# Hashed attention and two feed-forward blocks on one core: products of weights and VectorE rows change places within a step

## The chip, the core and the metric

The kernel runs on one core of a Trainium2 chip. The metric is the device time in microseconds of one execution. Four compute engines matter here: TensorE (PE, with its weight loads PEld), VectorE (DVE), ScalarE (ACT) and GpSimd (POOL, which here issues DMAs); SyncE (SP) issues the other DMAs. In the trace each engine takes its instructions in the order in which the program lists them, and waits where an operand or a buffer is not ready.

## The reference

Sixteen attention heads (2 batches of 8) over 768 positions with 64 features come first. Queries and keys are hashed to six bits by the signs of a projection; a score counts only where both hashes agree. Then two feed-forward blocks follow on the 1536 tokens with 512 features.

```python
q_bucket, k_bucket = hash(q @ proj), hash(k @ proj)      # 6 sign bits each
scores = where(q_bucket[:, None] == k_bucket[None, :], scale * q @ k.T, -1e9)
attn = exp(scores - scores.max(-1)); attn = attn / (attn.sum(-1) + 1e-9)
x = (attn @ v)                                           # to 1536 x 512
h = x @ w_in; x = (h * tanh(softplus(h))) @ w_out        # 512 -> 2048 -> 512
out = ((x @ w1) * (x @ w2)) @ w3 @ w_out2                # 512 -> 1024 -> 512
```

The large weights arrive as 64-bit floats and are decoded on the chip by one ScalarE and three VectorE operations. Products are made from high and low halves, three matmuls for each.

## The kernel before

The attention part is a hand-written pipeline of steps numbered n = 0, 1, 2, ...; six steps make a group j, and 96 steps (`NS`) hold all scores. A step makes the scores of 128 queries of one head against all 768 keys. What a step issues is fixed by a table `slots`, which `at(n, where, fn)` fills and `run(n, where)` empties, in the order in which the loop (L865 on) names the places. `pin` then ties each engine's instructions to this order, so within the attention part the order on an engine is that of the loop, nearly word for word.

The places and what stands in them:

- `scores` (L533): four matmuls into `ts`, one of two PSUM slots with the tag `s`. `tqk`, `tb` and `w3p` take slots of the same two. `maxima` (L549): VectorE's row maximum of `ts` and a small operation on it. `expo` (L559): ScalarE's exp of `ts` into `E`, with the row sums; it frees the slot.
- `un`: two units a step. A `unit` (L602) is three transposes of `E` into one of two PSUM buffers `et` and a copy to SBUF (`etf`), the first of a step on ScalarE, the second on VectorE (in steps with n mod 6 = 5 both are ScalarE's). `av` (L615): the product with v, into `pv`, in steps with n mod 6 = 2, 3, 4.
- `lv`: VectorE's work that others wait for: `bits_dve` (L506, the mask rows `qa` and `ka` out of `tb`), `norm` (L572, two small operations on the row sums, in steps with n mod 6 = 0), `w3_lo` (L688), `x_out` (L628).
- `pe`: other work of TensorE: `qk_transpose` (`tqk`), `bits_mm` (`tb`; that of q in steps 4, that of k in steps 5 of six), `rb_mm` (L582, `rb`, which spreads the reciprocals that `norm` left, in steps 0 of six), `w3_trans` (`w3p`, steps 24, 30, ..., 66), and two fillers that wait for none of these: `wp_mm` (L697, `wacc`: the product of w3 and w_out2, 24 matmuls a group, spread over steps 26 to 73 by `MM`, six of them in each step 5 of six and four in each step 0 of six) and `h_early` (L352, `hps`: the first matmuls of the feed-forward part, from step 83).
- `la`, `ea`, `ev`, `dm`: ScalarE's and VectorE's other work (splits, decoding, the copies `rb_act`, `w3_hi`, `h_keep`) and DMA issues.

After the last step the feed-forward part runs under a list `prog`; there the framework's scheduler chooses the order on each engine.

Of the kernel before, what the change touches and what calls it, by code (L numbers as in the profile page):

```python
# [34 lines left out]
def kernel(  # L35
# [292 lines left out]
    def h_half(n, j, f, o, m0=0, m1=None):  # L328
        w, xh = weight(n, "wi", j), xhl[n]
        m1 = 3 * KD if m1 is None else m1  # L330
        for m in range(m0, m1):
            kk, i = divmod(m, 3)
            ws, xs = PASS[i]
            nc.tensor.matmul(  # L334
                o, lhsT=w[:, ws, kk, f * 128:(f + 1) * 128], rhs=xh[xs][:, kk, :],
                start=(m == 0), stop=(m == 3 * KD - 1),
            )
# [14 lines left out]
    def h_early(n, j, f, m0, m1):  # L352
        if m0 == 0:
            wh[0] = ps.tile([128, 512], F32, tag="w", name="hps1")
        h_half(n, j, f, wh[0], m0, m1)
# [193 lines left out]
    def maxima(j, i):  # L549
        s = stats[j % 3]  # L550
        nc.vector.tensor_reduce(  # L551
            out=s[:, i, 1:2], in_=sc[j, i][:, :, 0:HS], axis=AX.XY, op=ALU.max, negate=True
        )
        nc.vector.scalar_tensor_tensor(  # L554
            out=s[:, i, 2:4], in0=s[:, i, 1:2].to_broadcast([128, 2]), scalar=THR,
            in1=s[:, i, 0:2], op0=ALU.is_le, op1=ALU.mult,
        )
# [14 lines left out]
    def norm(j):  # L572
        s = stats[j % 3]
        nc.vector.tensor_scalar(
            out=s[:, :, 4], in0=s[:, :, 4], scalar1=1e-9, scalar2=None, op0=ALU.add
        )
        nc.vector.reciprocal(out=s[:, :, 5], in_=s[:, :, 4])
# [74 lines left out]
    def pre_a(nm, i):  # L652
        pre[nm, i] = decode_a(pre[nm, i])
# [43 lines left out]
    def wp_mm(f, n0, n1):  # L697
        if n0 == 0:
            wacc[f] = ps.tile([128, 512], F32, tag="w", name="wacc")
        for n in range(n0, n1):  # L700
            g, s = divmod(n, 3)
            ws, rs = PASS[s]
            nc.tensor.matmul(  # L703
                wacc[f], lhsT=w3t[f][:, ws, g, :], rhs=wo2[rs][:, g, :],
                start=(n == 0), stop=(n == 3 * GT - 1),
            )
# [6 lines left out]

    slots = {}

    def at(n, where, fn):
        slots.setdefault((n, where), []).append(fn)

    def run(n, where):
        for fn in slots.pop((n, where), []):
            fn()
# [28 lines left out]
    for j in range(NJ):  # L752
        s = 6 * j
        for m in range(3):
            for kt in (2 * m, 2 * m + 1):
                at(s + 4 + m, "un", lambda j=j, kt=kt: unit(j, 0, kt))
                at(s + 7 + m, "un", lambda j=j, kt=kt: unit(j, 1, kt))
                at(s + 8 + m, "av", lambda j=j, kt=kt: av(j, kt))
        at(s + 6, "lv", lambda j=j: norm(j))
        at(s + 6, "pe", lambda j=j: rb_mm(j))  # L760
        at(s + 7, "la", lambda j=j: rb_act(j))
        at(s + 11, "lv", lambda j=j: x_out(j))
# [7 lines left out]
    for f in range(GT):  # L770
        n = 24 + 6 * f
        na, nb, nc_ = (n - 6, n - 4, n - 3) if f else (17, 20, 21)
        at(na, "ea", lambda f=f: pre_a(3, f))
        at(nb, "ev", lambda f=f: pre_b(3, f))
        at(nc_, "ev", lambda f=f: pre_c(3, f))
        at(n, "pe", lambda f=f: w3_trans(f))
        at(n + 1, "la", lambda f=f: w3_hi(f))
        at(n + 1, "lv", lambda f=f: w3_lo(f))
        m = 0
        for k_ in range(n + 2, n + 8):  # L780
            m1 = m + MM[k_ % 6]
            at(k_, "pe", lambda f=f, m=m, m1=m1: wp_mm(f, m, m1))
            m = m1
        assert m == 3 * GT
        at(n + 8, "la", lambda f=f: wp_out(f))
# [20 lines left out]
    n = 83  # L806
    for jj in range(3):
        for f in range(2):
            m = 0
            while m < 12:  # L810
                m1 = min(12, m + (4 if n % 6 in (2, 3, 4) or n == 83 else 8))
                at(n, "pe", lambda jj=jj, f=f, m=m, m1=m1: h_early(0, jj, f, m, m1))
                m = m1
                n += 1
            at(n, "la", lambda jj=jj, f=f: h_keep(0, jj, f))
# [49 lines left out]
    for n in range(max(NS + 6, HEND + 2)):  # L865
        j, i = divmod(n, 6)
        mark = len(nc.cur_bb.bb.instructions)
        run(n, "pr")
        if n < NS:
            scores(j, i)  # L870
        run(n, "la")
        if n < NS:
            maxima(j, i)
        run(n, "un")
        run(n, "av")
        run(n, "lv")
        if n < NS:
            expo(j, i)
        if n == 0:
            for x in range(2):  # L880
                with tc.issue_after(next(
                    i for i in reversed(nc.cur_bb.bb.instructions) if i.engine == nc.scalar.engine
                )):
                    pre_load(x)
        for w in ("pe", "ea", "ev", "dm"):
            run(n, w)
        pin(mark)
# [164 lines left out]
```

## Time and profile before

| | |
|---|---|
| runs | 916.21 us median of 3 (915.81 to 922.91) |
| profiled execution | 920.4 us, its span 918.6 us |
| TensorE busy | 830.0 us, 90% of the span |
| VectorE busy | 512.4 us, 56% |
| ScalarE busy | 459.9 us, 50% |
| mean granted TensorE clock | 0.953 of full speed |

The span runs from the first to the last instruction of the core. A busy TensorE is a matmul in flight, and matmuls overlap, so rows of a run of matmuls are best read from the start of one group to the start of the next. The granted clock has two levels, full (2.4 GHz, written 1.00) and half (1.2 GHz); a stretch with 0.80 was at half for four tenths of its time.

### The profile page before, as it was taken

How to read it: one execution, taken by the hardware profiler on the slowest of the kernel's cores; microseconds unless marked ns; L12 is line 12 of the kernel's file. 1: busy time of each engine (PE TensorE's matmuls, PEld its weight loads, DVE VectorE, ACT ScalarE, POOL GpSimd, SP SyncE). 2: the span in 40 equal slices, each digit the busy share in tenths (PEclk: the TensorE clock that was granted, in tenths of full speed). 3: DMA queues.
4: the chain of work that ended last, by engine and by line, in shares of the span. 5: the costliest groups of instructions: out<-in, count | busy, mean ns of one | idle time of the engine just before them, and what ended most of it. 6: DMA issues, size and time to landing. Idle time of an engine off the chain costs nothing.

```text
span 918.6 us, 10516 instructions
## 1 busy us (share of the span) xinstructions
PE 830.0 (90%) x4145; PEld 648.7 (71%) x4145; DVE 512.4 (56%) x711; ACT 459.9 (50%) x691; POOL 74.6 (8%) x131
## 2 busy tenths in 40 slices
PE   6778868888888898788999999999999999999998
PEld 4655656566666666556778778888888888888886
DVE  5477756666655756767689877432354434334321
ACT  4556645566645675657856554333344323334221
POOL 1000000000000000001022211100101101110000
PEclk8588979999999999999999999999999999999999
DMA  5112313131031331326098864424233224232101
GB/s 177 52 54 81 117 55 107 67 118 58 26 113 55 118 103 36 115 89 214 9 329 301 293 231 183 142 94 152 95 110 97 92 92 137 95 107 75 46 24 47
DMA packets 34594, 103.46 MB, mean 113 GB/s; under 512 B 3184, under 2 KB 11632, under 8 KB 33520
## 3 DMA queue, kind: packets, MB, share of 16 engines
q0 software_dynamic: 20928, 81.80, 26.3%
q1 hardware_dynamic: 13472, 20.85, 6.6%
q8 instruction: 33, 0.54, 0.2%
q14 instruction: 17, 0.14, 0.1%
q10 hardware_dynamic: 144, 0.13, 0.0%
HBM read 81.79 MB, written 20.97 MB: 112 GB/s over the span
## 4 chain that ended last, share of the span: by engine, by line
PE 71%; DVE 14%; issue 5%; DMA 5%; ACT 4%; POOL 1%; SPq 0%; ACTq 0%; DVEq 0%; POOLq 0%
PE abp L941 14%; PE hps L334 10%; PE x2a L914 10%; PE ts L540 8%; PE oac L965 7%; PE pv L620 6%; PE wacc L703 5%; DVE st L551 4%; PE et L605 4%; PE tb L500 3%; DMA raw<-in_moe_w_dram 2%; PE rb L587 2%; DMA raw<-in_moe_w_out_dram 2%; DVE qa L509 2%; DVE ka L509 2%
## 5 line engine op out<-in xcount | busy, mean ns | idle before, releaser
L551 DVE TENSOR_REDUCE st<-ts 128x1 f32<-128x768 f32 x96 | 91.9, 957 | 151.3 <-PE ts L540 151.3
L941 PE MATMUL abp<-x2hl,hl 128*128 128x512 f32 x576 | 139.3, 398 | 2.1 <-ACT mh L347 2.1
L334 PE MATMUL hps<-xhl,hl 128*128 128x512 f32 x552 | 135.8, 400 | 0.0
L914 PE MATMUL x2a<-ghl,hl 128*128 128x512 f32 x552 | 130.6, 394 | 1.2 <-DVE ghl L379 1.1
L941 PEld LDWEIGHTS abp<-x2hl,hl 128*128 128x128 f32 x576 | 109.4, 190 | 28.4 <-ACT mh L347 2.5
L269 DVE TENSOR_TENSOR hl<-f,hl 128x1024 fp32r<-128x1024 f32 x60 | 73.4, 1224 | 91.5 <-ACT hl L264 91.5
L334 PEld LDWEIGHTS hps<-xhl,hl 128*128 128x128 f32 x552 | 104.2, 191 | 26.6 <-issue 3.5
L914 PEld LDWEIGHTS x2a<-ghl,hl 128*128 128x128 f32 x552 | 103.6, 188 | 25.9 <-DVE ghl L379 2.0
L562 ACT ACTIVATE E<-ts,st 128x768 f32<-128x768 f32 x96 | 95.3, 993 | 27.9 <-DVE st L554 26.5
L612 ACT COPY etf<-et 128x384 f32<-128x384 f32 x112 | 51.9, 478 | 85.0 <-PE et L605 84.4
L605 PE MATMUL et<-ident,E 128*128 128x128 f32 x576 | 85.0, 287 | 0.0
L605 PEld LDWEIGHTS et<-ident,E 128*128 128x128 f32 x576 | 74.4, 149 | 4.5 <-ACT etf L612 0.2
L264 ACT CAST hl<-f 128x1024 fp32r<-128x1024 f32 x60 | 62.8, 1047 | 28.9 <-PE abp L941 12.0
L620 PE MATMUL pv<-etf,rv 128*64 128x384 f32 x384 | 74.5, 511 | 0.0
L540 PE MATMUL ts<-ka,qa 76*128 76x384 f32 x192 | 59.2, 393 | 12.7 <-ACT E L562 10.9
L965 PE MATMUL oac<-hl,phl 128*128 128x512 f32 x288 | 69.8, 393 | 0.0
L965 PEld LDWEIGHTS oac<-hl,phl 128*128 128x128 f32 x288 | 54.2, 188 | 12.4
L703 PE MATMUL wacc<-wo,w3t 128*128 128x512 f32 x192 | 56.8, 419 | 0.0
L950 DVE TENSOR_TENSOR asb<-abp,asb 128x512 f32<-128x512 f32 x24 | 16.6, 692 | 71.6 <-ACT asb L949 71.6
L949 ACT COPY asb<-abp 128x512 f32<-128x512 f32 x24 | 14.1, 586 | 83.9 <-PE abp L941 83.9
L89 ACT ACTIVATE g<-raw 128x1024 f32<-128x1024 f32 x36 | 41.0, 1140 | 28.5 <-DMA raw<-in_moe_w_dram 9.6
L540 PE MATMUL ts<-kb,qb 128*128 128x384 f32 x192 | 54.3, 367 | 0.0
(108 smaller groups left out, 965.2 us busy)
## 6 DMA issues: line engine op xcount, KB each, us to landing
raw<-in_moe_w_dram POOLq DMA_DIRECT2D x16, 1024.0 KB, 6.1
raw<-in_moe_w_out_dram POOLq DMA_DIRECT2D x12, 1024.0 KB, 8.2
raw<-in_moe_w_in_dram POOLq DMA_DIRECT2D x8, 1024.0 KB, 6.8
f<-keep_wi POOLq DMA_DIRECT2D x16, 512.0 KB, 3.7
f<-keep_wo POOLq DMA_DIRECT2D x16, 512.0 KB, 3.7
f<-wp_d POOLq DMA_DIRECT2D x12, 512.0 KB, 4.0
keep_wi<-g POOLq DMA_DIRECT2D x8, 512.0 KB, 4.2
keep_wo<-g POOLq DMA_DIRECT2D x8, 512.0 KB, 3.1
```

The source lines that it names most:

```text
L264: nc.scalar.copy(out=hl[:, 0], in_=f)
L269: nc.vector.tensor_sub(out=hl[:, 1], in0=f, in1=hl[:, 0])
L334: nc.tensor.matmul(o, lhsT=w[:, ws, kk, f * 128:(f + 1) * 128], rhs=xh[xs][:, kk, :], start=(m == 0), stop=(m == 3 * KD - 1),)
L540: nc.tensor.matmul(t[:, a, 0:HS], lhsT=l[0:kk, qt * 128:(qt + 1) * 128], rhs=r[0:kk, a * HS:(a + 1) * HS], start=(l is qa), stop=(l is qb),)
L551: nc.vector.tensor_reduce(out=s[:, i, 1:2], in_=sc[j, i][:, :, 0:HS], axis=AX.XY, op=ALU.max, negate=True)
L562: nc.scalar.activation(out=e.rearrange("p (a n) -> p a n", a=2), in_=sc.pop((j, i))[:, :, 0:HS], func=AF.Exp, scale=s[:, i, 2:3], bias=s[: ...
L605: nc.tensor.transpose(t[:, ci * 128:(ci + 1) * 128], E[j, e * CH + ci][:, kt * 128:(kt + 1) * 128], ident,)
L620: nc.tensor.matmul(pv[j][e * D:(e + 1) * D, 0:HS], lhsT=raws[p, "v"][:, e, kt, :], rhs=eth.pop((j, e, kt)), start=(kt == 0), stop=(kt == C ...
L703: nc.tensor.matmul(wacc[f], lhsT=w3t[f][:, ws, g, :], rhs=wo2[rs][:, g, :], start=(n == 0), stop=(n == 3 * GT - 1),)
L914: nc.tensor.matmul(x2a[n][d], lhsT=w[:, ws, f, d * 128:(d + 1) * 128], rhs=g[:, gs, f, :], start=(j == 0 and f == 0 and s == 0), stop=(j = ...
L941: nc.tensor.matmul(t[:, i, :], lhsT=ws_[i][:, ws, kk, (f % 2) * 128:(f % 2) * 128 + 128], rhs=xh[:, xs, kk, :], start=(m == 0), stop=(m == ...
L965: nc.tensor.matmul(oac[n][t], lhsT=g[:, gs, t * 128:(t + 1) * 128], rhs=w[:, ws, f % 2, :], start=(f == 0 and s == 0), stop=(f == FF2 // 1 ...
```

## The change

The order of places in a step is altered. `norm` gets a place of its own (`nm`), and `nm` and `lv` run right after the maxima, ahead of `un`. The fillers `wp_mm` and `h_early` get a place `mm` after `av` and ahead of `pe`. No instruction is added or taken away.

```diff
-        at(s + 6, "lv", lambda j=j: norm(j))
+        at(s + 6, "nm", lambda j=j: norm(j))
...
-            at(k_, "pe", lambda f=f, m=m, m1=m1: wp_mm(f, m, m1))
+            at(k_, "mm", lambda f=f, m=m, m1=m1: wp_mm(f, m, m1))
...
-                at(n, "pe", lambda jj=jj, f=f, m=m, m1=m1: h_early(0, jj, f, m, m1))
+                at(n, "mm", lambda jj=jj, f=f, m=m, m1=m1: h_early(0, jj, f, m, m1))
...
         run(n, "la")
         if n < NS:
             maxima(j, i)
+        run(n, "nm")
+        run(n, "lv")
         run(n, "un")
         run(n, "av")
-        run(n, "lv")
+        run(n, "mm")
         if n < NS:
             expo(j, i)
```

TensorE in a step 5 of six (here 29), before: units, then the mask product of k (`tb<-kb`), then six products of weights (`wacc`), then the next scores.

```order
L605 MATMUL et<-ident,E 128x128 x6
L500 MATMUL tb<-kb,psel 76x384 x4
L703 MATMUL wacc<-wo_0_108,w3t 128x512 x2
L703 MATMUL wacc<-wo_1_109,w3t 128x512
L703 MATMUL wacc<-wo_0_108,w3t 128x512 x2
L703 MATMUL wacc<-wo_1_109,w3t 128x512
L540 MATMUL ts<-ka,qa 128x384 x2
```

The same place in the changed kernel:

```order
L605 MATMUL et<-ident,E 128x128 x6
L703 MATMUL wacc<-wo_0_108,w3t 128x512 x2
L703 MATMUL wacc<-wo_1_109,w3t 128x512
L703 MATMUL wacc<-wo_0_108,w3t 128x512 x2
L703 MATMUL wacc<-wo_1_109,w3t 128x512
L500 MATMUL tb<-kb,psel 76x384 x4
L540 MATMUL ts<-ka,qa 128x384 x2
```

The six products of weights have moved ahead of the mask product.

TensorE in the step after (30, a step 0 of six), before: units, `rb`, four products of weights, the transposes of a w3 block (`w3p`), the next scores.

```order
L605 MATMUL et<-ident,E 128x128 x6
L587 MATMUL rb<-ident,st 64x128 x6
L703 MATMUL wacc<-wo_0_108,w3t 128x512 x2
L703 MATMUL wacc<-wo_1_109,w3t 128x512
L703 MATMUL wacc<-wo_0_108,w3t 128x512
L678 MATMUL w3p<-ident,g 128x128 x8
L540 MATMUL ts<-ka,qa 128x384 x2
```

The same place in the changed kernel:

```order
L605 MATMUL et<-ident,E 128x128 x6
L703 MATMUL wacc<-wo_0_108,w3t 128x512 x2
L703 MATMUL wacc<-wo_1_109,w3t 128x512
L703 MATMUL wacc<-wo_0_108,w3t 128x512
L587 MATMUL rb<-ident,st 64x128 x6
L678 MATMUL w3p<-ident,g 128x128 x8
L540 MATMUL ts<-ka,qa 128x384 x2
```

Here `rb` has moved behind the four products.

VectorE in a step 0 and the step 1 after it (24 and 25), before: maximum, small operation, unit's copy (`etf`), mask rows of k (`ka`), the two operations of `norm` (L574, L577); in the next step the copy, then `w3_lo` (L689).

```order
L551 TENSOR_REDUCE st<-ts 128x1
L554 SCALAR_TENSOR_TENSOR st<-st 128x2
L612 COPY etf<-et 128x384
L509 TENSOR_SCALAR ka<-tb,ccol 12x768
L574 TENSOR_SCALAR st<-st 128x6
L577 RECIPROCAL st<-st 128x6
L551 TENSOR_REDUCE st<-ts 128x1
L554 SCALAR_TENSOR_TENSOR st<-st 128x2
L612 COPY etf<-et 128x384
L689 TENSOR_TENSOR w3t<-w3p,w3t 128x1024
```

The same place in the changed kernel:

```order
L551 TENSOR_REDUCE st<-ts 128x1
L554 SCALAR_TENSOR_TENSOR st<-st 128x2
L574 TENSOR_SCALAR st<-st 128x6
L577 RECIPROCAL st<-st 128x6
L509 TENSOR_SCALAR ka<-tb,ccol 12x768
L612 COPY etf<-et 128x384
L551 TENSOR_REDUCE st<-ts 128x1
L554 SCALAR_TENSOR_TENSOR st<-st 128x2
L689 TENSOR_TENSOR w3t<-w3p,w3t 128x1024
L612 COPY etf<-et 128x384
```

`norm` is now first behind the maximum, then the mask rows, and the unit's copy is last; `w3_lo` is ahead of the copy too. In steps 5 of six VectorE has no unit's copy, so its order there is as before. At the end of the attention part the scheduler also places things otherwise: of 24 matmuls of the feed-forward part, 20 stood between the last units before and 4 stand there now, and some loads and stores on POOL's queue change places.

## Rows read from the trace of the kernel before

**Rows 1.** Stretches: us, busy of PE, PEld, DVE, ACT, POOL, clock, DMA share, GB/s.

```profile
0.00:455.00 455.00, 373.70 (x2174) 281.64 (x2175) 289.79 (x480) 275.13 (x474) 18.35 (x37) 0.91 0.26 89
455.00:600.00 145.00, 141.77 (x616) 112.11 (x615) 107.51 (x112) 74.94 (x85) 29.69 (x47) 0.99 0.68 237
...
500.00:520.00 20.00, 20.00 (x87) 15.94 (x85) 18.63 (x18) 11.28 (x11) 5.66 (x10) 1.00 0.87 303
```

**Rows 2.** TensorE's waits in the attention part: us in total, times, longest.

```profile
PE rb L587 <- DVE st L577: 35.6, 14, 2.8
PE tb L500 <- DVE qa L509: 25.5, 13, 3.3
PE ts L540 <- ACT E L562: 10.9, 13, 2.5
```

**Rows 3.** Timeline of TensorE, step 36: start, us, instruction, [idle before <-releaser].

```profile
177.16 0.52 PE L540 MATMUL ts<-ka,qa 76*128 76x384 f32 x2
...
177.87 0.81 PE L605 MATMUL et<-ident,E 128*128 128x128 f32 x6
181.26 0.88 PE L587 MATMUL rb<-ident,st 128*64 128x128 f32 x12 [2.58 <-DVE st L577]
182.07 1.19 PE L703 MATMUL wacc<-wo,w3t 128*128 128x512 f32 x4
183.10 1.03 PE L678 MATMUL w3p<-ident,g 128*128 128x128 f32 x8
183.89 0.60 PE L540 MATMUL ts<-ka,qa 76*128 76x384 f32 x2
```

**Rows 4.** Timeline of VectorE, steps 36 and 37.

```profile
179.14 0.55 DVE L612 COPY etf<-et 128x384 f32<-128x384 f32 x1
179.70 1.07 DVE L509 TENSOR_SCALAR ka<-tb,ccol 12x768 fp32r<-12x768 f32 x1
180.81 0.17 DVE L574 TENSOR_SCALAR st<-st 128x6 f32<-128x6 f32 x1
...
186.42 1.21 DVE L689 TENSOR_TENSOR w3t<-w3p,w3t 128x1024 fp32r<-128x1024 f32 x1
```

**Rows 5.** Timeline of ScalarE, step 36: the end of the exp.

```profile
180.14 0.19 ACT L562 ACTIVATION_READ_ACCUMULATOR E<-ts,st 128x1 f32 x1
```

**Rows 6.** Timeline of TensorE and VectorE, step 41.

```profile
199.23 0.52 PE L540 MATMUL ts<-ka,qa 76*128 76x384 f32 x2
...
201.33 1.07 DVE L509 TENSOR_SCALAR qa<-tb,ccol 12x768 fp32r<-12x768 f32 x1
...
202.55 0.89 PE L500 MATMUL tb<-kb,psel 128*76 128x384 f32 x4 [1.79 <-DVE qa L509]
203.28 1.54 PE L703 MATMUL wacc<-wo,w3t 128*128 128x512 f32 x6
204.66 0.52 PE L540 MATMUL ts<-ka,qa 76*128 76x384 f32 x2
```

**Rows 7.** Stretches from maximum to maximum: steps 24, 36, 54, 72, 84, 90.

```profile
118.74:126.26 7.52, 5.34 (x32) 4.58 (x31) 3.12 (x6) 2.26 (x4) 0.00 (x0) 0.56 0.03 10
178.06:184.88 6.82, 4.24 (x36) 3.57 (x35) 3.03 (x6) 3.76 (x6) 0.00 (x0) 1.00 0.00 0
...
260.55:268.98 8.43, 5.85 (x36) 5.01 (x35) 3.04 (x7) 4.06 (x6) 0.00 (x0) 0.80 0.08 27
...
347.70:355.06 7.36, 4.78 (x28) 3.85 (x27) 3.03 (x7) 2.04 (x4) 0.00 (x0) 0.77 0.00 0
...
398.70:407.07 8.37, 5.79 (x32) 4.64 (x31) 3.03 (x6) 2.63 (x5) 0.00 (x0) 0.80 0.00 0
424.33:433.01 8.68, 5.84 (x32) 4.70 (x31) 4.56 (x8) 3.22 (x7) 1.31 (x2) 0.80 0.35 107
```

**Rows 8.** Timeline of ScalarE, step 90: the copy that frees the buffer of `hps`.

```profile
425.12 0.59 ACT L361 COPY mh<-hps 128x512 f32<-128x512 f32 x1
```

**Rows 9.** The page's DMA issues: KB each, median us to landing.

```profile
raw<-in_moe_w_out_dram POOLq DMA_DIRECT2D x12, 1024.0 KB, 8.2
```

## The prediction

> **What bounds the kernel now.** I cut the span into stretches first. The attention part, up to about 455 us, keeps TensorE busy for 373.70 of 455.00 us at a granted clock of 0.91; the stretch behind it holds it busy for 141.77 of 145.00 us [rows 1]. So TensorE sets the end throughout, but only the first part leaves it idle time to win. The list of waits says for what it idles there: 35.6 us in 14 waits for `rb`, which needs the reciprocals of `norm`; 25.5 us in 13 waits for the mask product of k, which needs VectorE to have read the PSUM slot of q's; and 10.9 us where scores wait for the exp [rows 2]. The timeline of one group of six then shows the first two close together, in a step 5 and the step 0 after it.
>
> In step 36 [rows 3], counted from its first scores at 177.16, the units' transposes stand at 0.71 and take 0.81, so TensorE is done with them at 1.52. Then it idles 2.58 us until `rb` at 4.10; behind `rb` come four products of weights at 4.91, `w3p` at 5.94, and the next scores at 6.73. Those four products need nothing of `rb`. VectorE meanwhile [rows 4] copies the unit at 1.98, makes the mask rows at 2.54, and comes to `norm` at 3.65. In step 41 [rows 6], the mask product stands at 3.32 after 1.79 us idle, since `qa` runs until 3.17; the six ready products come after it at 4.05, and the next scores at 5.43.
>
> **The change, step by step.** Steps 5 of six. Six products take 203.28 to 204.66, 1.38 us or 0.23 each [rows 6]. Placed after the units they run from about 1.52 to 2.90, inside the idle time; the mask product still comes at 3.32, takes 0.73, and the next scores start at 4.05 instead of 5.43. Gain 1.38, with 0.4 us of the stall left. There are eight such steps (29, 35, ..., 71). Step 83 has four matmuls of `hps` instead, 0.9. Sum 12.0. The bounds of each are nothing (if something else holds the scores) and the whole stall of 1.79; I take the length of what moves in, because `qa` doesn't move. What hides the rest is nothing: the stall that stays is counted.
>
> Steps 0 of six with products of weights. `norm` moves ahead of the copy and the mask rows, that is from 180.81 to 179.14, by 1.67 [rows 4]; so `rb` can start at 4.10 - 1.67 = 2.43. The four products, 4 x 0.23 = 0.92, fill 1.52 to 2.44. So `rb` starts at about 2.43, lasts 0.81 [rows 3] to 3.24. `w3p` takes the slot that the exp frees; the exp's last part ends at 180.33, which is 3.17 [rows 5], so `w3p` isn't held, and 0.79 later, at 4.03, the next scores start. They need the slot of `ka`, which is done at about 1.98 + 0.45 (`norm`, from its start at 180.81 to `rb`) + 1.07 = 3.50. Gain 6.73 - 4.03 = 2.70 in each of the steps 30, 36, 42, 48: 10.8.
>
> In steps 54, 60, 66 the same work takes longer: 8.43 us from maximum to maximum against 6.82, with a granted clock of 0.80 against 1.00 [rows 7] (one of three stands there). The clock falls to half in the stretch that holds both stalls and the matmuls behind them run at half speed. With the stalls filled, I expect it to stay: 2.70 + 1.61 = 4.31 each, 12.9. Step 72 has no `w3p`: it takes 7.36 now and would end with `rb`, at 3.24: 4.1. Sum of this kind 27.8.
>
> The Trainium skill's page "TensorE: Matmul & The Clock Gate" (section "What's actually happening") has it that the array's clock is throttled by default and that activity releases it. By that rule the half clock of these steps goes with their idle time and the sum is 55.1, as below; by the rows' clock left as it is, 45.6.
>
> Steps 0 without products (12, 18, 78). Only `norm` moves: `rb` ends at 3.24 instead of 4.91, and the next scores wait for the exp's end at 3.17 at most. Gain 1.67 each, 5.0. Step 24 has a `w3p` and a clock of 0.56 over 7.52 us [rows 7]: between 1.67 and 7.52 - 4.1 = 3.4, I take 2.4. In step 6 the mask product itself stands ahead of `rb`, and I count nothing. Sum 7.4.
>
> Steps 84 and 90, where `hps` fills. Step 84: eight matmuls, 1.84, from 1.52 to 3.36, then `rb` to 4.17; now 8.37 at 0.80 [rows 7]: 4.2. In step 90 the eight matmuls take a buffer that ScalarE's copy frees at 425.71 [rows 8], 1.4 us after the maximum began [rows 7], so some 2.3 after the scores (a maximum starts 0.9 after them, as in step 36); so 2.3 + 1.84 + 0.81 = 4.95 of now 8.68: 3.7. Sum 7.9.
>
> What the change costs. VectorE's copy of the unit now stands behind `norm` and `ka` (16 groups) or behind `w3_lo` (8 groups), and the second unit of the next step needs its PSUM buffer. In step 36 the copy would end at 1.98 + 0.45 + 1.11 + 0.55 = 4.09; that second unit starts at 4.03 + 0.71 + 0.4 = 5.1. In step 37 `w3_lo` [rows 4] puts it 1.21 later, to end some 3.8 after the scores; the next step's second unit comes no earlier than 3.17 + 1.1 = 4.3. So both are hidden, by 1.0 and 0.5 us; if that cover is gone, TensorE waits for each microsecond beyond. DMA issues move with their steps and no queue gets another wait there.
>
> At the end of the attention part 16 matmuls fewer lie between the last units, which wait for VectorE's copies: between nothing and 16 x 0.23 = 3.7 us; I take 1.5, since the copies come earlier on VectorE too.
>
> **The sum.** 12.0 + 27.8 + 7.4 + 7.9 = 55.1, less 1.5 is 53.6. The profiled execution took 920.4 us (span 918.6 and 1.8 around it): 866.8. The runs' median, 916.21, is 4.2 lower. I don't take that off as well, since an execution in which the clock fell less often would explain the difference, and then less of the clock's part is there to win. Forecast 867.
>
> **A rule that speaks against it.** "Perfetto Trace Analysis" of the Trainium skill (section "Optimization Strategy", on consistent bubbles) says that the same gap repeating on the engine that should be full can mean too few buffers for the next tile. The 13 waits of the mask product are that: two slots, and the one it needs is read by VectorE. By the rule another order wouldn't free the slot sooner. That is so (3.32 stays 3.32); a mask product that doesn't come sooner is a rival below, with its price from rows.
>
> **Rivals.** *The feed-forward part gives back.* Behind the attention part VectorE is busy 18.63 of 20.00 us and the DMA engines 0.87 [rows 1], and loads and stores there are ordered anew. For it: little slack. Against: the same work follows the same end. If one or two loads of 8.2 us [rows 9] come late in full, 875 to 883. Chance 0.12.
>
> *The clock still falls.* Then 3 x 1.61 in steps 54 to 66 is missing, 1.5 in step 72 (7.36 less 4.91, four products and 0.1), and 1.6 each in steps 84 and 90, as in 54: 9.5 in all, 876. For it: in step 24 it is at half nearly throughout, at 0.56 [rows 7]. Against: in step 36 the full idle time left it at 1.00. Chance 0.06.
>
> *The mask product holds the scores after all.* Filling its wait gains nothing if the scores behind it wait for another release; the 10.9 us that they wait for the exp now [rows 2] speak for it. But 4.05 is later than the exp's 3.17. Without the 12.0: 879. Chance 0.05.
>
> *Slower, by the copies.* Where `norm`, mask rows or `w3_lo` run late, the unit's copy behind them is late, and with it the transposes of the next step, in 24 steps. It decides against the change where the copies come more than 53.6 / 24 = 2.2 us beyond their mean cover (16 at 1.0, 8 at 0.5: 0.8). At 3.5 us late each, 24 x 2.7 = 65: 932. For it: `w3_lo` waits for ScalarE. Against: `w3_lo` started right behind the copy before, waiting for nothing. Chance 0.03.
>
> *No change.* The order is pinned and shows the new rows, so the change does what it says; some wait that the trace doesn't name would have to take its place everywhere, 916. Chance 0.02.
>
> **Chances and range.** The forecast has 0.72. Its own spread is the bounds of step 24, of the join and of the steps of 54 to 90, about 857 to 876; to 884 the range takes in the three faster rivals. So 857 to 884. About 1% is what a measurement of this kernel can tell from no change: faster 0.95, within it 0.02, slower 0.03.
>
> **What would show it.** `rb`'s waits fall from 35.6 to under 8 us, what is left in the steps without products; the mask product's from 25.5 to about 14, eight of them at 0.4. Step 36 lasts about 4.1 and step 41 about 4.05. The stretch of steps 54 to 72 shows a clock of 1.00. The feed-forward part keeps its length. It would be wrong if `et` waits for VectorE's copy, if scores wait for the exp in steps 0 and 5, or if TensorE idles in the feed-forward part.

## The result and the profile after

The changed kernel takes 859.32 us, the median of four runs (858.76 to 860.92); the kernel before took 919.56 us in the four runs beside it (915.81 to 923.48). The ratio is 0.9347, with an interval of 0.9294 to 0.9401. The profiled execution took 859.71 us, 60.7 less than the 920.4 of before; the forecast gain was 53.6, and 867 the forecast time.

Where the time came from is read first by stretches of the program, cut where a maximum begins (of the first step, of steps 30 and 72, and the last one). Columns are us, busy time of PE, PEld, DVE, ACT and POOL, the granted clock, the DMA share and GB/s. The kernel before:

```profile
12.50:150.58 138.08, 105.92 (x559) 77.99 (x558) 88.26 (x140) 80.30 (x142) 3.60 (x6) 0.79 0.24 81
150.58:347.70 197.12, 166.52 (x1038) 127.61 (x1037) 120.10 (x197) 118.18 (x205) 4.94 (x8) 0.97 0.23 78
347.70:447.10 99.40, 84.21 (x489) 62.48 (x488) 66.53 (x109) 64.30 (x111) 6.40 (x10) 0.93 0.30 103
447.10:918.60 471.50, 464.16 (x2022) 373.42 (x2020) 229.74 (x242) 191.90 (x228) 56.21 (x94) 0.99 0.40 134
```

The changed kernel, the same four stretches:

```profile
12.49:139.07 126.58, 97.11 (x555) 70.23 (x556) 87.86 (x139) 79.34 (x141) 3.61 (x6) 0.87 0.25 85
139.07:303.90 164.83, 161.93 (x1038) 121.80 (x1037) 120.11 (x196) 114.93 (x205) 4.96 (x8) 1.00 0.29 95
303.90:388.30 84.40, 78.46 (x490) 57.06 (x489) 66.44 (x109) 64.27 (x111) 6.42 (x10) 1.00 0.36 122
388.30:857.90 469.60, 463.67 (x2022) 373.57 (x2020) 230.89 (x242) 191.29 (x228) 56.75 (x94) 1.00 0.39 134
```

The second stretch, steps 30 to 71, gives 32.3 us. TensorE issues the same 1038 matmuls there, and is now busy for 161.93 of 164.83 us at a full clock: almost nothing is left to win in it. Steps 72 to 95 give 15.0. The first stretch gives 11.5 (it begins 0.6 us ahead of the first maximum in the row of before; from that maximum, at 13.10, it is 10.9), and the feed-forward part, behind the last maximum, 1.9.

TensorE's waits in the attention part (us in total, times, longest) answer to [rows 2]:

```profile
PE tb L500 <- DVE qa L509: 13.5, 13, 3.3
PE ts L540 <- ACT E L562: 9.2, 13, 1.6
PE rb L587 <- DVE st L577: 2.7, 4, 0.9
```

`rb` waits for 2.7 us instead of 35.6, the mask product for 13.5 instead of 25.5, and the scores wait for the exp no longer than before. Step 36 and VectorE's end of step 37, which answer to [rows 3 to 5]:

```profile
161.70 0.52 PE L540 MATMUL ts<-ka,qa 76*128 76x384 f32 x2
162.42 0.82 PE L605 MATMUL et<-ident,E 128*128 128x128 f32 x6
162.99 1.17 PE L703 MATMUL wacc<-wo,w3t 128*128 128x512 f32 x4
163.69 0.17 DVE L574 TENSOR_SCALAR st<-st 128x6 f32<-128x6 f32 x1
164.12 1.07 DVE L509 TENSOR_SCALAR ka<-tb,ccol 12x768 fp32r<-12x768 f32 x1
164.14 0.87 PE L587 MATMUL rb<-ident,st 128*64 128x128 f32 x12
164.69 0.19 ACT L562 ACTIVATION_READ_ACCUMULATOR E<-ts,st 128x1 f32 x1
164.94 1.09 PE L678 MATMUL w3p<-ident,g 128*128 128x128 f32 x8
165.22 0.56 DVE L612 COPY etf<-et 128x384 f32<-128x384 f32 x1
165.79 0.60 PE L540 MATMUL ts<-ka,qa 76*128 76x384 f32 x2
...
166.58 0.81 PE L605 MATMUL et<-ident,E 128*128 128x128 f32 x6
...
168.98 0.55 DVE L612 COPY etf<-et 128x384 f32<-128x384 f32 x1
...
170.00 0.82 PE L605 MATMUL et<-ident,E 128*128 128x128 f32 x6
```

Counted from the scores at 161.70, the four products stand at 1.29, `rb` at 2.44, `w3p` at 3.24 and the next scores at 4.09. No row of TensorE in between carries a wait. `rb` at 2.44 has its products just done (2.46) and its reciprocals just there (the second operation of `norm` ends at 164.09, which is 2.39): both came at the same time. The unit's copy, now last on VectorE, ends at 4.08; the next step's second unit, three of the six transposes further, starts at about 166.58 + 0.41, which is 5.29.

Step 41, which answers to [rows 6]:

```profile
181.21 0.51 PE L540 MATMUL ts<-ka,qa 76*128 76x384 f32 x2
182.48 1.62 PE L703 MATMUL wacc<-wo,w3t 128*128 128x512 f32 x6
183.29 1.07 DVE L509 TENSOR_SCALAR qa<-tb,ccol 12x768 fp32r<-12x768 f32 x1
184.51 0.90 PE L500 MATMUL tb<-kb,psel 128*76 128x384 f32 x4 [0.41 <-DVE qa L509]
185.25 0.52 PE L540 MATMUL ts<-ka,qa 76*128 76x384 f32 x2
```

The six products fill the wait, 0.41 us of it is left, and the mask product stands at 3.30 as before.

### The profile page after: what moved, and what is told of

The parts are those of the page before. It is cut to its first block, busy times and chain, and to the rows that moved or that the text cites. A ratio compares the mean times of both kernels' runs of the same rounds, so it can differ in the third digit from the quotient of the medians.

```text
span 857.9 us, 10511 instructions
## 1 busy us (share of the span) xinstructions
PE 811.0 (95%) x4145; PEld 630.0 (73%) x4145; DVE 513.1 (60%) x711; ACT 455.7 (53%) x691; POOL 75.2 (9%) x131
## 4 chain that ended last, share of the span: by engine, by line
PE 76%; DVE 12%; ACT 5%; issue 3%; DMA 3%; POOL 0%; ACTq 0%; DVEq 0%; POOLq 0%
PE abp L944 16%; PE hps L334 12%; PE x2a L917 11%; PE oac L968 8%; PE ts L540 8%; PE pv L620 6%; PE et L605 4%; PE wacc L703 4%; DVE st L551 4%; PE tb L500 3%; DVE qa L509 2%; DMA raw<-in_moe_w_dram 2%; ACT E L562 2%; PE rb L587 2%; PE tqk L470 1%
## 5 line engine op out<-in xcount | busy, mean ns | idle before, releaser
L944 PE MATMUL abp<-x2hl,hl 128*128 128x512 f32 x576 | 137.5, 395 | 0.0
L334 PE MATMUL hps<-xhl,hl 128*128 128x512 f32 x552 | 133.2, 395 | 0.8 <-ACT mh L361 0.8
L334 PEld LDWEIGHTS hps<-xhl,hl 128*128 128x128 f32 x552 | 102.9, 188 | 26.3 <-issue 2.4
L605 PE MATMUL et<-ident,E 128*128 128x128 f32 x576 | 82.3, 280 | 0.1
L605 PEld LDWEIGHTS et<-ident,E 128*128 128x128 f32 x576 | 71.1, 144 | 5.6 <-DVE etf L612 0.8
L540 PE MATMUL ts<-ka,qa 76*128 76x384 f32 x192 | 56.1, 374 | 15.2 <-ACT E L562 9.2
L379 DVE TENSOR_TENSOR ghl<-mh,ghl 128x1024 fp32r<-128x1024 f32 x24 | 29.3, 1223 | 38.9 <-ACT ghl L378 38.9
```

The lines of the kernel that those rows point to most:

```text
L334: nc.tensor.matmul(o, lhsT=w[:, ws, kk, f * 128:(f + 1) * 128], rhs=xh[xs][:, kk, :], start=(m == 0), stop=(m == 3 * KD - 1),)
L540: nc.tensor.matmul(t[:, a, 0:HS], lhsT=l[0:kk, qt * 128:(qt + 1) * 128], rhs=r[0:kk, a * HS:(a + 1) * HS], start=(l is qa), stop=(l is qb),)
L605: nc.tensor.transpose(t[:, ci * 128:(ci + 1) * 128], E[j, e * CH + ci][:, kt * 128:(kt + 1) * 128], ident,)
L944: nc.tensor.matmul(t[:, i, :], lhsT=ws_[i][:, ws, kk, (f % 2) * 128:(f % 2) * 128 + 128], rhs=xh[:, xs, kk, :], start=(m == 0), stop=(m == ...
```

## Experiments

All kernels below are made from the changed kernel unless a diff says otherwise. Times are medians of four runs, set beside the 859.32 of the changed kernel. The kernel before had medians of 915.21 to 919.56 us beside the different groups of kernels, so medians of two groups compare to some 4 us, and what is smaller is read from steps. Lengths of steps are from the start of one maximum to the start of the next.

### The two halves of the change

`fillers_only` leaves the fillers where the change puts them, and moves VectorE's rows back behind the unit's copy:

```diff
-        at(s + 6, "nm", lambda j=j: norm(j))
+        at(s + 6, "lv", lambda j=j: norm(j))
...
-        run(n, "nm")
-        run(n, "lv")
         run(n, "un")
         run(n, "av")
+        run(n, "lv")
         run(n, "mm")
```

> Only the products of weights move (ahead of the mask product and of rb); VectorE keeps its old order. My theory: in steps 5 of six the whole 1.38 us comes, eight times, and 0.93 in step 83: 12.0. In steps 0 rb still starts at 4.10 us after the scores, so the four products fill part of its wait and the step ends at about 5.7 to 5.8 us instead of 6.8, and if the clock stays at full in steps 54 to 66, 2.5 us less there. With steps 72, 84 and 90 some 33 us in all: 887 us. If the fillers alone make the gain, 860; if VectorE's order alone makes it, 915 or more.

Measured: 886.99 us, as expected. `vector_rows_only` does the other half and puts `wp_mm` and `h_early` back in their old place:

```diff
-            at(k_, "mm", lambda f=f, m=m, m1=m1: wp_mm(f, m, m1))
+            at(k_, "pe", lambda f=f, m=m, m1=m1: wp_mm(f, m, m1))
...
-                at(n, "mm", lambda jj=jj, f=f, m=m, m1=m1: h_early(0, jj, f, m, m1))
+                at(n, "pe", lambda jj=jj, f=f, m=m, m1=m1: h_early(0, jj, f, m, m1))
```

> Only VectorE's order changes (sums, mask rows and w3's low half ahead of the unit's copy); the products of weights stay behind the mask product and rb. My theory: the mask product's wait of 1.79 us stays in all thirteen steps, rb comes at 2.43 us after the scores, and with the four products behind it a step 0 lasts about 5.0 us; together with the steps that have no products some 38 us less than before: 882 us. If VectorE's order alone makes the gain, 860; if the fillers alone make it, 918 or more.

Measured: 885.16 us, 3 above the 882 expected; steps 65 and 71 were partly at half clock in the profiled execution and took 1.55 longer each. The kernel before had 915.92 beside these, so the halves give 28.9 and 30.8 us, and the whole gives 56.6 against that figure: they nearly add up. The waits of `fillers_only`:

```profile
PE rb L587 <- DVE st L577: 23.5, 13, 2.6
PE tb L500 <- DVE qa L509: 13.5, 13, 3.3
```

and of `vector_rows_only`:

```profile
PE tb L500 <- DVE qa L509: 25.5, 13, 3.3
PE rb L587 <- DVE st L577: 12.5, 15, 2.4
```

The mask product's wait depends on the fillers alone (13.5 with them ahead, 25.5 without). `rb`'s needs both: 35.6 falls to 23.5 with the fillers, to 12.5 with `norm` ahead, to 2.7 with both.

Two more kernels split the half on VectorE. `norm_ahead_only` leaves only `norm` ahead of the copy; mask rows and `w3_lo` are behind it again:

```diff
         run(n, "nm")
-        run(n, "lv")
         run(n, "un")
         run(n, "av")
+        run(n, "lv")
```

> As the changed kernel, but only the two operations on the row sums stand ahead of the unit's copy on VectorE; mask rows and w3's low half stand behind it again. My theory: rb needs those two alone, the scores behind it wait for mask rows that end at 4.1 us instead of 3.5, which is when the scores come anyway: 859 to 862 us. If the mask rows and the low half ahead of the copy carry a part of the gain, 865 or more.

Measured: 860.81 us (860.22 to 861.59). Steps 30 to 71 have the lengths of the changed kernel to 0.04 us. So putting the mask rows and `w3_lo` ahead of the copy brought nothing there, and cost nothing. `norm_behind_mask` puts `norm` behind the mask rows, still ahead of the copy:

```diff
-        at(s + 6, "nm", lambda j=j: norm(j))
+        at(s + 6, "lv", lambda j=j: norm(j))
```

> As the changed kernel, but the two operations on the row sums stand behind the mask rows (both still ahead of the unit's copy). My theory: rb comes 1.1 us later, at 3.54 us after the scores, which the four products cover only to 2.44: each step 0 from 12 on that has a mask product lasts 1.1 us longer, in twelve of them some 13 us: 873 us. If the products cover rb's wait whatever the order on VectorE, 860.

Measured: 876.99 us. Steps 30 to 66 last 5.39 instead of 4.16, and `rb` waits for 16.8 us. The 1.07 us row ahead of `norm` costs 1.23 in each step. It is the place of `norm` that counts, to the row. The total is 4 above the 873 expected: steps 30 to 71 cost 8.6 us, and the first 30 steps and steps 72 to 95 another 8.9, where the clock fell as well (step 78 lasts 5.91 at 0.50, against 3.33 at 1.00).

### The fillers of one kind of step

`fillers_step5_only` keeps the products ahead only in steps 5 of six:

```diff
-            at(k_, "mm", lambda f=f, m=m, m1=m1: wp_mm(f, m, m1))
+            at(k_, "mm" if k_ % 6 == 5 else "pe", lambda f=f, m=m, m1=m1: wp_mm(f, m, m1))
```

> The changed kernel, but only the six products of weights of a step 5 of six stay ahead of the mask product; those of the other steps are behind rb again. The feed-forward part's matmuls stay ahead. Theory (the products of a step 0 fill the time up to rb, 0.92 us): rb starts at 2.43 as before, the four products follow it, and the seven steps 30 to 66 last 0.9 us longer; step 72 ends with rb and its four products, 0.9 longer too: 8 x 0.9 = 7.4 over the changed kernel, 865 to 868. Steps 5 stay at 4.05. Rival (the products delay rb itself as much as they fill): 859 to 861.

Measured: 865.36 us. Steps 30 to 66 last 5.13 instead of 4.16 and step 72 4.26 instead of 3.34, so four products of 0.23 are worth 0.97 and 0.92 there, as the theory said. Steps 5 stay at 4.05. The first 30 steps took 123.84 us here and 126.58 in the changed kernel. Of this difference 1.0 lies ahead of step 26, where the programs are the same; it returns below.

### The rest of the mask product's wait

`mask_rows_first` puts q's mask rows ahead of the maximum in steps 5 of six:

```diff
-        at(n1 + 1, "lv", lambda: bits_dve(u, nm))
+        at(n1 + 1, "pr" if nm == "q" else "lv", lambda: bits_dve(u, nm))
```

> The changed kernel, and q's mask rows come ahead of the maximum in steps 5 of six instead of behind it. Theory (what is left of step 5 is the wait of k's mask product for those rows, 13.5 us in 13 waits): the rows are done about 1.3 us after the scores instead of 3.2, the mask product follows the six products at 2.90, the next scores start at 3.6 instead of 4.05 in the eight steps with products, and when the exp is done, at about 3.5, in the five without: 8 x 0.42 and 5 x 0.5, some 6 us, 853 to 855, and the waits of 13.5 us are gone. Rival (the exp, which now comes later because its maximum stands behind the rows, takes the place of the wait): 858 to 861, with the same time in waits of scores for the exp.

Measured: 856.96 us (854.49 to 858.65), 2.4 less, between the two ranges expected. Its ratio to the kernel before, 0.9347 (0.9311 to 0.9382), is that of the changed kernel, so the time alone doesn't show a gain; the steps do. Its waits, and TensorE's and VectorE's rows of step 41, whose scores stand at 179.49:

```profile
PE ts L540 <- ACT E L562: 16.6, 20, 1.6
PE tb L500 <- DVE qa L509: 4.1, 3, 2.1
```

```profile
179.69 1.07 DVE L509 TENSOR_SCALAR qa<-tb,ccol 12x768 fp32r<-12x768 f32 x1 [0.67 <-PE tb L500]
182.22 0.86 PE L500 MATMUL tb<-kb,psel 128*76 128x384 f32 x4
183.11 0.30 PEld L540 LDWEIGHTS ts<-ka,qa 76*128 76x128 f32 x2 [0.40 <-ACT E L562]
183.11 0.62 PE L540 MATMUL ts<-ka,qa 76*128 76x384 f32 x2
```

The mask product stands at 2.73 without a wait and the next scores at 3.62, as expected. But steps 4 and 5 together shrink only from 7.98 to 7.68: the maximum, now behind the rows, starts 0.4 later, and the weight load of the scores behind waits 0.40 for the exp. Steps 30 to 71 take 162.80 us instead of 164.83. In steps without products the exp takes all of it: steps 76 and 77 last 7.62 instead of 7.70, and steps 16 and 17 last 8.15 instead of 7.67 (in `norm_ahead_only`, where they were at full clock as here; 8.03 in the changed kernel with step 17 at 0.89), as the maximum there starts 1.2 us later. Waits of 9.4 us for the mask rows went, and 7.4 us of waits for the exp came. So both answers hold, each in its kind of step: the theory in the steps with products, at 0.3 instead of 0.42, and the rival in those without, where the edit costs up to 0.5.

### The late copy, the slower rival

`w3_rows_double` and `w3_rows_triple` run VectorE's row of `w3_lo` two and three times, with the same result, ahead of the copy of steps 1 of six (the edit of the first; the second has `range(3)`):

```diff
-        nc.vector.tensor_sub(
-            out=w3t[f][:, 1].rearrange("p (a g) n -> p a (g n)", a=2),
-            in0=spare_ps.pop((f, "w3")),
...
+        t = spare_ps.pop((f, "w3"))
+        for _ in range(2):
+            nc.vector.tensor_sub(
+                out=w3t[f][:, 1].rearrange("p (a g) n -> p a (g n)", a=2),
+                in0=t,
...
```

> The changed kernel, with VectorE's 1.22 us row of w3 (w3_lo) run twice, which puts the unit's copy behind it 1.22 us later in eight steps 1 of six. Theory (in step 37 the copy ends 0.87 us before the next step's second unit wants its buffer): 0.35 us uncovered in each of eight steps, 2.8 us, so 861 to 863, with short waits of the units for VectorE's copy. Rival (the copies have more slack than that, or none of it lies on the path): 859 to 860. Rival (the late maximum behind the copy delays the exp and so the scores as well): 8 x 1.22 and more, 869 or above.

> The same with w3_lo run three times: the copy comes 2.44 us later. Theory of a cover of 0.87 us: 8 x 1.57 = 12.6 us over the changed kernel, 871 to 873, with eight waits of the units for VectorE's copy of some 1.6 us. Rival (no cost on the path): 859 to 861. Rival (VectorE cannot catch up within the group and the delay adds up over several steps): 880 or above.

Measured: 867.24 and 869.68 us. Step 38 of the kernel with two:

```profile
173.89 0.49 PE L605 MATMUL et<-ident,E 128*128 128x128 f32 x3
174.12 0.55 DVE L612 COPY etf<-et 128x384 f32<-128x384 f32 x1
174.72 0.55 PE L605 MATMUL et<-ident,E 128*128 128x128 f32 x3 [0.34 <-DVE etf L612]
175.20 1.51 PE L620 MATMUL pv<-etf,rv 128*64 128x384 f32 x8
```

The added row takes 1.22 us and 0.34 of it comes out as a wait, so the cover was 0.88, as read from the rows of step 37 (0.87; the forecast had 0.5). The wait costs more than itself: steps 1 and 2 of a group together last 7.99 instead of 7.42, 0.57 more. The products with v start 1.31 us after the first transpose (173.89 to 175.20); in the changed kernel they start 0.74 after it (170.00 to 170.74), with the six transposes in one run. Over steps 30 to 71 this is 168.85 us instead of 164.83, 4.0 more, and 0.5 in steps 25 and 26, where the theory had 2.8 in all. The profiled executions differ by 8.7 (spans of 866.7 and 857.9); of the other 4.2, 2.8 lie ahead of step 25, where the programs don't differ, and 1.4 behind step 71.

With three rows the wait has another place:

```profile
174.62 0.48 ACT L612 COPY etf<-et 128x384 f32<-128x384 f32 x1 [0.46 <-PE et L605]
...
175.16 0.55 PE L605 MATMUL et<-ident,E 128*128 128x128 f32 x3 [0.57 <-ACT etf L612]
175.59 0.55 DVE L612 COPY etf<-et 128x384 f32<-128x384 f32 x1
```

The second unit of step 38 starts at 175.16, ahead of VectorE's copy of step 37 at 175.59. So it isn't in the buffer that this copy frees: it waits for ScalarE's copy of the first unit of its own step, at 0.57. With so long a row the framework dealt out the two `et` buffers in another order when the program was built: in steps 26, 32, ..., 68 both units have the same buffer, while the changed kernel takes the two in turn throughout. Over steps 30 to 71 the cost is 7.7 us, 1.10 a group, instead of the 1.57 forecast. Of the 1.10, 0.80 lies between the units and the products with v, and 0.3 ahead of the scores of step 39, which start 0.06 after the exp's end: the late maximum, of which a rival of the kernel with two spoke, plays a part here. The range expected of this kernel was missed for this reason, that of `w3_rows_double` for the dearer wait and for the 4.2 us elsewhere. The wait and the cover are shown; the price of a copy that comes much later is not.

### The clock of the first 30 steps

From the first maximum to that of step 25 the programs of four kernels are the same, and yet they took 102.9 us (changed), 102.2 (`fillers_step5_only`), 105.4 and 105.0 (the two above). Step 6 alone lasts 5.05 in two of them and 6.58 and 6.65 in the others. Four kernels fill idle time of the first 26 steps with matmuls of zeros, whose products nobody reads; the first leaves the changed kernel's order as it is:

```diff
+    def idle_mm(n):
+        t = ps.tile([128, 512], F32, tag="w", name="idle")
+        for _ in range(n):
+            nc.tensor.matmul(t, lhsT=zr[:, 0:128], rhs=zr, start=True, stop=True)
+
+    for n, c in ((5, 6), (11, 6), (17, 6), (23, 6), (25, 8)):
+        at(n, "mm", lambda c=c: idle_mm(c))
```

> The changed kernel with 32 matmuls of zeros added, whose products nobody reads: six each in steps 5, 11, 17 and 23, where k's mask product waits, and eight in step 25, where scores wait 2.5 us for the first w3 block. Open is why the steps ahead of 30 gained more than forecast and differ from kernel to kernel (126.6 us from the first maximum to that of step 30 in the changed kernel, 123.8 to 129.6 in kernels that differ only behind step 25). Theory (idle time in these steps brings the half clock, and the half clock stretches the steps after it): filled, steps 7 to 30 show a clock near 1.00, step 26 lasts 3.6 us instead of 6.37, step 11 about 4.0 instead of 5.25; some 5 us less, 853 to 856. Rival (the clock there follows something else): the clock of steps 6 to 30 stays at 0.88 to 0.97, and the time at 858 to 862.

Measured: 857.65 us (854.20 to 859.39), between the two ranges expected. Steps 25 and 26 of the changed kernel, and then steps 25 and 26 and steps 6 to 11 of this one:

```profile
115.39:126.54 11.15, 8.64 (x38) 5.71 (x37) 7.44 (x10) 5.76 (x12) 0.54 (x1) 0.69 0.25 94
```

```profile
118.40:126.48 8.08, 7.40 (x46) 5.43 (x45) 7.26 (x10) 5.75 (x12) 0.54 (x1) 1.00 0.23 71
...
39.78:70.03 30.25, 25.35 (x128) 17.68 (x127) 20.07 (x31) 14.67 (x27) 0.71 (x1) 0.75 0.12 42
```

With eight matmuls more, steps 25 and 26 are 3.07 us shorter, at a clock of 1.00 instead of 0.69. From step 13 on the clock is full. But steps 6 to 11 were at half for half of their time in this run, and give 2.4 back (30.25 against 27.86). In their runs the two kernels overlap, so the time doesn't settle whether the filler helps. Nor do steps 25 and 26: `mask_rows_first` has the 38 matmuls of the changed kernel there, without filler, and is as short, at full clock.

```profile
116.83:124.91 8.08, 5.57 (x38) 4.04 (x37) 7.28 (x11) 5.77 (x12) 0.54 (x1) 1.00 0.21 65
```

Both steps are at 1.00 in all four kernels with the eight matmuls and in two of the ten without (`norm_behind_mask` is the other). So full clock is worth 3.07 us here, and that the filler brings it is likely but not shown.

`mask_first_idle_filled` has the order of `mask_rows_first` and four, four, four, four and eight of these matmuls in the same steps.

> q's mask rows ahead of the maximum, as in mask_rows_first, and matmuls of zeros added: four each in steps 5, 11, 17 and 23, eight in step 25. Theory (both gains stand beside each other: the mask product's wait is gone, and the half clock of steps 11, 12, 23 and 24 in mask_rows_first goes with the idle time): 852 to 855. Rival (the clock follows something else): 856 to 858.

Measured: 855.53 us (852.14 to 857.18), just over the range of the theory. The clock is 1.00 in steps 5 to 23, but 0.66 in step 24 and 0.61 in step 78, which nothing fills. `first_steps_filled` adds four to each of steps 0 to 3:

```diff
-    for n, c in ((5, 4), (11, 4), (17, 4), (23, 4), (25, 8)):
+    for n, c in ((0, 4), (1, 4), (2, 4), (3, 4), (5, 4), (11, 4), (17, 4), (23, 4), (25, 8)):
```

> The kernel mask_first_idle_filled with four more matmuls of zeros in each of steps 0 to 3, which run at half clock with TensorE idle for half of their time. Theory (idle time brings the half clock there too): the clock of steps 1 to 4 rises to 1.00 and these 18 us shrink by 2 to 3 us, as far as TensorE and not the other engines set them: 850 to 853. Rival (the steps wait for VectorE and ScalarE, and the added matmuls, 1.84 us a step at half clock, come in their way): 854 to 860.

Measured: 853.55 us (851.89 to 855.75), between the two ranges and overlapping with the kernel it is made from. Steps 0 to 3 of the changed kernel, and steps 0 to 3 and 4 to 5 of this one:

```profile
12.49:30.90 18.41, 10.44 (x38) 7.66 (x39) 7.65 (x12) 9.16 (x17) 0.00 (x0) 0.59 0.08 28
```

```profile
13.00:29.37 16.37, 10.08 (x54) 7.81 (x53) 7.65 (x12) 8.78 (x17) 0.00 (x0) 1.00 0.06 22
29.37:38.18 8.81, 8.28 (x40) 7.37 (x38) 4.76 (x9) 7.43 (x13) 0.00 (x0) 0.61 0.39 134
```

Sixteen matmuls more, and the four steps are 2.0 us shorter, at full clock. The fall comes later, in steps 4 and 5, which nothing fills, and costs 1.1 us there. So the theory holds for steps 0 to 3 in this kernel. Step 1 is at 1.00 in both kernels with this filler, and at 0.50 to 0.54 in the twelve without. The last kernel of the study tries to better it. It has q's mask rows ahead of the maximum only in the steps with products, and more of these matmuls:

```diff
-        at(n1 + 1, "pr" if nm == "q" else "lv", lambda: bits_dve(u, nm))
+        at(n1 + 1, "pr" if nm == "q" and 29 <= n1 + 1 <= 71 else "lv", lambda: bits_dve(u, nm))
...
-    for n, c in ((0, 4), (1, 4), (2, 4), (3, 4), (5, 4), (11, 4), (17, 4), (23, 4), (25, 8)):
+    for n, c in ((0, 4), (1, 4), (2, 4), (3, 4), (4, 4), (5, 6), (11, 6), (17, 6), (23, 6), (25, 8)):
```

> As first_steps_filled, with three edits: q's mask rows stay ahead of the maximum only in steps 29 to 71 (the steps 5 with products of weights), four matmuls of zeros are added in step 4, and steps 5, 11, 17 and 23 have six instead of four. Theory (in steps without products the rows ahead of the maximum delay the exp by more than they gain: at full clock steps 16 and 17 lasted 8.16 us with them and 7.66 without, steps 22 and 23 8.89 and 8.39; and the half clock of steps 4 and 5, 1.1 us, goes with their idle time): 2 x 0.5 in these steps, up to 0.8 in step 24, up to 1.1 in steps 4 and 5, so 850 to 852.5. Rival (the halves of the clock only move to other steps, and the rows' place is worth nothing): 853 to 856.

Measured: 854.56 us (852.35 to 855.21), no better than `first_steps_filled`. Steps 12 to 24 of that kernel, and then steps 12 to 24 and steps 0 to 3 of this one:

```profile
63.26:113.18 49.92, 41.73 (x272) 29.95 (x271) 39.79 (x66) 34.22 (x61) 1.82 (x3) 0.97 0.28 95
```

```profile
65.60:113.68 48.08, 40.79 (x276) 29.70 (x275) 39.80 (x65) 34.35 (x61) 1.82 (x3) 1.00 0.29 101
...
12.42:31.18 18.76, 12.47 (x54) 9.81 (x53) 7.65 (x12) 8.77 (x17) 0.00 (x0) 0.78 0.09 33
```

Where the rows stand behind the maximum again, 1.8 us are won, as the theory said: 0.5 in steps 16 and 17, and 1.3 in steps 22 to 24, part of which is the clock (0.69 in step 24 before, now 1.00). But the half clock, which was in steps 4 and 5, now stands in steps 2 to 4 and in 7 and 8, though steps 0 to 3 hold the same matmuls in both kernels: 2.4 us are lost in steps 0 to 3 alone. So these two kernels have less half clock (a mean of 0.985 to 0.993 in their runs, against 0.975 to 0.981 in the changed kernel), and the filler doesn't decide where the rest of it falls, as the rival said. That the rows' place is worth nothing, which it said as well, does not fit the 0.5 of steps 16 and 17.

Of all kernels here `first_steps_filled` has the lowest median: its four runs all lie below the four of the changed kernel, by 5.8 us in the median. Their ratios to the kernel before, 0.9293 (0.9223 to 0.9364) and 0.9347 (0.9294 to 0.9401), overlap, because the kernel before itself ran from 912.26 to 924.78 beside them.

## Why the prediction was right, and where it was off

The mechanism came as forecast, with the time of the kernel, 859.32, near the fast end of the range. The gain of the profiled executions is 7.1 us larger than the 53.6 of the sum: 3.8 more ahead of step 30, 3.4 more behind the last maximum, 0.4 more in steps 72 to 95, 1.1 less in steps 30 to 71 (32.3 against 33.4), and 0.6 ahead of the first maximum. About half of the first two is not the change's own, as the paragraphs on them show.

**Steps 5 of six** (forecast 1.38 each, 12.0 in all). Steps 29 to 71 went from 5.42 to 4.05, 1.375 each; step 83 from 4.97 to 4.04, 0.93. Right, and `vector_rows_only` shows that nothing else brings it: its steps 5 stay at 5.43, or 6.98 where the clock falls.

**Steps 0 with products** (forecast 27.8). Steps 30 to 48 gave 2.65 each (2.70), steps 54, 60 and 66 gave 4.27, 4.05 and 4.26 (4.31), step 72 gave 4.02 (4.1). Each place in step 36 came within 0.06 us: `rb` at 2.44 (2.43), `w3p` at 3.24 (3.24), the next scores at 4.09 (4.03). The clock of steps 30 to 71 is 1.00, so the rival in which it still falls is out. The Trainium skill's page "TensorE: Matmul & The Clock Gate", section "What's actually happening", says that the throttled clock is the default and activity releases it; these steps and the filled first steps agree, 0.97 to 1.00 and 0.59 to 1.00; the 0.78 of the same filled steps in `filled_rows_first_late` shows that more goes into it than how many matmuls a step holds.

**What lies ahead of step 30** (forecast 7.1: 1.67, 1.67 and 2.4 in steps 12, 18 and 24, nothing in step 6, and 1.38 in step 29). Measured 10.9: 2.26, 1.83, 3.36, 1.83 in step 6, and 1.38. This is the term that was mis-sized, by 3.8 us. The step that failed is the clock of these steps: the forecast counted it in step 24 and put it at nothing in the others. "In step 6 the mask product itself stands ahead of `rb`, and I count nothing" holds for the order: at a clock of 0.61 step 6 lasts 7.05 us with `norm` in its old place (`fillers_only`) and 7.05 with it ahead (`vector_rows_only`). It lasts 5.05 in the changed kernel, at full clock, and 6.58 at 0.74 in `w3_rows_double`, whose program is the same up to there. So these 1.83 us are luck of one execution, and part of the rest may be: the same program took 102.2 to 105.4 us up to step 25, so the place of the clock's falls moves the time by some 3 us.

**Steps 78, 84 and 90.** 2.33, 4.16 and 3.38 against 1.67, 4.2 and 3.7. The stretch of steps 72 to 95 gave 15.0 against 14.6.

**The join** (forecast 1.5 lost, between nothing and 3.7). Nothing was lost. From the last maximum to the first product of the second matrix (`x2a`) it takes 17.1 us before, 17.0 in the changed kernel and 16.9 to 17.2 in the other four of the first group, whatever stands between the last units. The feed-forward part as a whole went from 471.5 to 469.6, and it has 471.1 in `fillers_only` and 469.0 to 469.4 in the other three. Cut at the same matmuls, its first 63.3 us and its last 356.4 are equal before and after; the 1.9 us lie in between. Before, and then changed:

```profile
510.45:562.20 51.75, 48.52 (x201) 38.49 (x200) 38.10 (x40) 25.55 (x31) 11.06 (x17) 0.97 0.74 254
```

```profile
451.60:501.50 49.90, 48.21 (x202) 38.74 (x201) 39.35 (x41) 27.44 (x33) 10.37 (x16) 0.97 0.75 265
```

TensorE is idle there for 3.2 us before and 1.7 after, in one to three waits for ScalarE and VectorE, with the DMA engines at 0.74 and 0.75; in `fillers_only` it is 3.8 and in `vector_rows_only` 1.3. Why these waits differ was not found, and nothing shows that the change shortens them. This, with the 1.5 that was not lost, is the other 3.4 us of the difference. The rival in which the feed-forward part gives the gain back is out.

**The mask product stays where it was** (3.32, now 3.30), as the rival said it might, and its wait is filled all the same: the scores behind it came at 4.04, and no exp held them. The rule that the prediction weighed (the Trainium skill, "Perfetto Trace Analysis", "Optimization Strategy": repeating gaps can mean too little buffer space for the next tile) fits the resource here, the slot that VectorE still reads. Work that was ready took most of the wait in the steps that have such work, 1.79 to 0.41 us, without another buffer, and 25.5 to 13.5 us over all. What was left of it went with an earlier reader instead, in `mask_rows_first`, and then the exp was next.

**The copies behind** hide as forecast, with more room: the copy of step 36 ends 1.2 us ahead of the next second unit (1.0 forecast), that of step 37 0.87 (0.5), and no unit waits for VectorE's copy between 139 and 304 us. The slower rival was far off. Its rate of 1 us for each us beyond the cover is not settled: 0.34 late cost 0.57 in `w3_rows_double`, and 1.57 late by this cover cost 1.10 in `w3_rows_triple`, where the buffers were dealt out otherwise.

**The base.** The forecast kept the 920.4 of the profiled execution. The kernel before had medians of 919.56, 915.92, 915.21, 917.90 and 919.50 here; so the choice of the base is worth up to 5 us, about as much as the terms that were off.

## What to carry to other kernels

Where an engine takes its work in order, look behind each wait that repeats for work that is ready already, and put it ahead of the waiting instruction: its length is the gain as long as the awaited result does not come sooner, and if the result can also come sooner by moving its producer ahead of a row that nobody waits for yet, the two gains nearly add up (here 28.9 and 30.8 us apart, 56.6 together). Before moving a row back on the other engine, read its cover (when it would end, and when its reader asks for it), since beyond the cover the copy's delay reaches the path (0.34 us late cost 0.57 here). Where half the clock stands behind a stall, count the stall and the slow work behind it together, and keep a range of some microseconds for stretches whose clock differs between executions.

## What was not expected of the hardware

- Matmuls that compute nothing can shorten a stretch: with sixteen more, steps 0 to 3 took 16.37 us instead of 18.41, at a granted clock of 1.00 instead of 0.59 (in another kernel with the same sixteen 18.76, at 0.78).
- Where the clock falls is not the same for the same instructions of TensorE. Steps 25 and 26 hold the same 38 matmuls in the changed kernel and in `mask_rows_first` and took 11.15 us at 0.69 and 8.08 at 1.00. In the kernel before steps 54, 60 and 66 were at 0.79 to 0.80 and steps 30 to 48 at 1.00; in `vector_rows_only`, where the wait of steps 5 remains, steps 65 and 71 fell and step 59 did not:

```profile
265.34:270.77 5.43, 3.64 (x22) 3.05 (x21) 2.75 (x5) 1.89 (x4) 0.00 (x0) 1.00 0.14 48
...
291.18:298.16 6.98, 5.19 (x22) 4.18 (x21) 2.75 (x4) 1.89 (x4) 0.00 (x0) 0.76 0.63 209
```

The same 22 matmuls take 3.64 us in step 59 and 5.19 in step 65. What decides between the two was not found.
- A wait of 0.34 us between two groups of transposes cost 0.57 in the length of the steps (`w3_rows_double`).
